# Low parts of a channel product's block operands: GpSimd in place of VectorE

## The chip, the cores and the metric

One core of one Trainium2 chip. The metric is device microseconds of the whole kernel on that core: 571.56 us is the median of three runs before the change (570.91 to 572.75).

## What is computed

A soft-capped attention over 4 batches and 12 heads, and a mixer on its output: one product along the tokens, then one along the channels.

```python
scores = scale * np.matmul(q, k.transpose(0, 1, 3, 2))
scores = cap * np.tanh(scores / cap)
attn = softmax(scores)                        # batch 4, heads 12, seq 448, head_dim 64
x = (attn @ v), heads side by side            # 4 x 448 x 768
h = np.maximum(xt @ w_tok1, 0.0) @ w_tok2     # along the tokens
u = x + h.transpose(0, 2, 1)
h2 = np.maximum(u @ w_ch1, 0.0) @ w_ch2       # along the channels, 768 -> 1536 -> 768
return u + h2
```

## The kernel before, in words

Precision comes from splitting: an operand of a large product is held as a high part (a rounded copy, `F32R`) and a low part (the operand less its high part), and each product is three matmuls, high by high, low by high and high by low (`TERMS`).

The channel product, the last 45% of the run, goes through 1536 hidden channels in `NG` = 6 groups of 256. For each group `ch1` multiplies a batch's `u` with the group's first weights into a PSUM tile, and ScalarE applies the ReLU. From group 1 on, two batches make a pair, named (group, half): (1,0), (1,1), (2,0) to (5,1), ten in all. The second product of a pair is written as seven block products of 3 x 3 matmuls each (`ch2_pair`, 63 matmuls at `L992`), which take sums and differences of the pair's hidden blocks as operands, in the manner of Strassen and Winograd. The names:

- `relu` (`L914`, ScalarE) writes two of the five buffers of `hid` for each batch. It overwrites what the pair before had there: for the first batch it waits for that pair's p4 and p2, for the second for its p5 and p3. It also frees the PSUM tile of `ch1`.
- `operands` and `form` (`L929`, GpSimd): four differences x, t1, t2 and t4 of `hid` blocks.
- `split`: for each of the seven operands p1 to p7 the high part (`L953`, ScalarE, out of `hid` into a ring of `NO` = 6 slots of `ops`) and the low part (`L958`, `hid` less the high part). A slot comes free when TensorE has read it. Products run in the order p1, p7, p6, p4, p5, p2, p3, in the last group p1, p2, p6, p7, p5, p4, p3.
- `ch2_pair`: its results accumulate in PSUM, and each product's running result is added into `u` by VectorE (`L1020` for two banks at once, `L1080` for one) before the chain's next product may write there. A ch2_pair starts when a PSUM tile of ring `a` is free, that of a ReLU of the pair behind it.
- `decode`: the next group's weights are loaded and rebuilt by VectorE and ScalarE in the same stretch: `L255` (ScalarE), `L261` and `L262`, `L268` and `L269` (VectorE); first weights then `L306` (ScalarE) and `L310` (VectorE); second weights `L281` to `L284` (VectorE, 128 columns each), `L289` and `L290` (ScalarE), `L298` and `L299` (VectorE).

TensorE does ch1 of two batches (72 matmuls) and then the ch2_pair of the pair before, in turn. So a pair's operands are made during the previous pair's ch2_pair and the next two ch1. The first pair, (1,0), has no pair before it: between its second ReLU and its ch2_pair stand two ch1 alone.

The order of each engine's instructions is fixed when the program is built: a planner (`Plan`) keeps a queue of jobs for each engine with a cost, and emits the job that could start first by its own clock. A job's cost thus sets the order of those around it. At run time each engine works strictly in that order and waits on semaphores.

`RELIEF` names the low parts that GpSimd makes. Before the change these are three, p2, p7 and p4 of the last pair (5,1); the other 67 of 70 are VectorE's.

Of the kernel before, what the change touches and what calls it, by code (L numbers as in the profile page):

```python
# [28 lines left out]
NG = FF // (GF * P)  # L29
# [20 lines left out]
    ("p3", 6, "h3", "a", 0, 1),  # L50
)
FINISH = tuple(PRODUCTS[n] for n in (0, 5, 2, 1, 4, 3, 6))
RELIEF = {(NG - 1, 1): ("p2", "p7", "p4")}

SWITCH = {("pv", "qk"): 200, ("qk", "bg"): 195, ("bg", "pv"): 147, ("qk", "pv"): 143, ("bg", "qk"): 199}
DRAIN = 250
# [49 lines left out]
class Plan:  # L106
# [27 lines left out]
    def job(self, engine, cost, took, emit, *deps, slack=0.0, key=None):  # L134
        deps += (self.pe if self.at is None else self.at,)
        j = Job(cost, took if engine in ("sp", "pool") else took + SIGNAL, emit, deps, slack)
        self.jobs[engine].append(j)
        if key is not None:
            self.done[key] = j
        return j  # L140
# [48 lines left out]
def tile_softcap_mixer(ctx, tc, qk, v, cap, w1, w2, wc1, wc2, out):  # L189
# [671 lines left out]
    while t < steps_in:  # L861
        n = 2 if PAIRED[0] <= t < PAIRED[1] else 1
# [60 lines left out]
    def operands(n, old):  # L923
        h = late["h"]
        place = {"h0": 0, "h1": 1, "t1": 2, "h3": 3, "x": 4, "t2": 0, "t4": 0}

        def form(key, out, a, b, *deps):
            e, cost = (nc.gpsimd, (1170, 1250)) if FORM == "gps" else (nc.vector, (536, 620))
            job(FORM, *cost, lambda: e.tensor_tensor(h[:, out], h[:, a], h[:, b], op=ALU.subtract),  # L929
                *deps, slack=500.0, key=("f", n, key))  # L930

        form("x", 4, 3, 2, ("r", n, 1), *([("s", old, "p7")] if old else []))
        form("t1", 2, 2, 0, ("f", n, "x"), ("r", n, 0))
        form("t2", 0, 3, 2, ("f", n, "t1"), ("s", n, "p1"))
        form("t4", 0, 1, 0, ("f", n, "t2"), ("s", n, "p6"))
        source = {"h0": ("r", n, 0), "h1": ("r", n, 0) if n[0] == NG - 1 else ("f", n, "t4"), "h3": ("f", n, "t2")}
        before = None
        for k, _, of, *_ in products(n):
            deps = [source.get(of, ("f", n, of)), room("o")] + ([("sh", n, before)] if before else [])
            split(n, k, h[:, place[of]], deps)  # L940
            before = k
# [2 lines left out]
        return FINISH if n[0] == NG - 1 else PRODUCTS  # L944

    def split(n, k, src, deps):
        on = "gps" if k in RELIEF.get(n, ()) else "dve"

        def high():
            i = len(rings["o"].holds) % NO  # L950
            t = late["o"][:, i]
            operand[n, k] = t, rings["o"].take(1)
            nc.scalar.activation(t[:, 0], src, AF.Copy)  # L953

        def low():
            t = operand[n, k][0]
            e = nc.vector if on == "dve" else nc.gpsimd
            e.tensor_tensor(t[:, 1], src, t[:, 0], op=ALU.subtract)  # L958

        job("act", 468, 568, high, *deps, slack=800.0, key=("sh", n, k))  # L960
        job(on, *((536, 620) if on == "dve" else (1170, 1250)), low, ("sh", n, k), slack=800.0, key=("s", n, k))
# [323 lines left out]
```

## Time and profile before

| | |
|---|---|
| median of three runs | 571.56 us (570.91 to 572.75) |
| profiled execution, its own time | 571.16 us |
| its span, first to last instruction | 569.4 us |
| TensorE busy | 561.8 us (99%), 3012 matmuls |
| VectorE busy | 491.4 us (86%) |
| ScalarE busy | 298.9 us (52%) |
| GpSimd busy | 61.0 us (11%) |
| chain that ended last | PE 85%, DVE 7%, ACT 3%, DMA 3% |

PE is TensorE's matmul, PEld its weight load, DVE is VectorE, ACT ScalarE, POOL GpSimd. A row of the chain is read as: start, length, what the end of the run was waiting for at that time. Where the chain shows PE, TensorE itself is what takes the time; where it shows another engine in the middle of the product, TensorE worked on something else then, but what it needed next was being made there.

### The profile page before, as it was taken

How to read it: one execution, taken by the hardware profiler on the slowest of the kernel's cores; microseconds unless marked ns; L12 is line 12 of the kernel's file. 1: busy time of each engine (PE TensorE's matmuls, PEld its weight loads, DVE VectorE, ACT ScalarE, POOL GpSimd, SP SyncE). 2: the span in 40 equal slices, each digit the busy share in tenths (PEclk: the TensorE clock that was granted, in tenths of full speed). 3: DMA queues.
4: the chain of work that ended last, by engine and by line, in shares of the span. 5: the costliest groups of instructions: out<-in, count | busy, mean ns of one | idle time of the engine just before them, and what ended most of it. 6: DMA issues, size and time to landing. Idle time of an engine off the chain costs nothing.

```text
span 569.4 us, 8201 instructions
## 1 busy us (share of the span) xinstructions
PE 561.8 (99%) x3012; PEld 431.8 (76%) x3012; DVE 491.4 (86%) x857; ACT 298.9 (52%) x415; POOL 61.0 (11%) x66
## 2 busy tenths in 40 slices
PE   8999999999999999999999999999999999999996
PEld 2333455544646799999999899999999999998995
DVE  2999999998999998637859899988999899959597
ACT  7999999899899443222234433334342424224230
POOL 0000100000000000000004202020202030303050
PEclk9999999999999999999999999999999999999999
DMA  7554767666451232000212223112220212010055
GB/s 244 174 157 117 236 193 230 208 205 203 112 167 34 70 108 75 0 2 0 75 38 74 75 55 93 37 39 74 75 69 7 83 66 75 0 39 0 3 195 193
DMA packets 26780, 55.50 MB, mean 97 GB/s; under 512 B 7024, under 2 KB 16752, under 8 KB 26736
## 3 DMA queue, kind: packets, MB, share of 16 engines
q1 hardware_dynamic: 24144, 48.21, 26.7%
q0 software_dynamic: 2160, 6.39, 3.9%
q8 instruction: 24, 0.39, 0.3%
q10 hardware_dynamic: 432, 0.34, 0.2%
q14 instruction: 20, 0.16, 0.1%
HBM read 47.97 MB, written 5.59 MB: 94 GB/s over the span
## 4 chain that ended last, share of the span: by engine, by line
PE 85%; DVE 7%; ACT 3%; DMA 3%; issue 1%; SPq 0%; DVEq 0%; ACTq 0%
PE ps_g L1033 28%; PE ps_o L992 21%; PE ps_pv L502 7%; PE ps_qk L424 6%; PE ps_h L660 6%; PE ps_u L683 5%; PE ps_o L1070 5%; PE ps_t L632 2%; PE ps_s L553 2%; PE ps_qk L435 1%; PE ps_pv L505 1%; ACT e L454 1%; DMA wraw<-in_w 1%; DVE ops L958 1%; ACT e L462 1%
## 5 line engine op out<-in xcount | busy, mean ns | idle before, releaser
L1033 PE MATMUL ps_g<-uhl,wc 128*128 128x448 f32 x648 | 137.3, 367 | 0.0
L992 PE MATMUL ps_o<-ops,wc 128*128 128x448 f32 x630 | 131.0, 367 | 0.8 <-ACT hid L914 0.5
L1033 PEld LDWEIGHTS ps_g<-uhl,wc 128*128 128x128 f32 x648 | 120.9, 188 | 11.2 <-issue 0.7
L992 PEld LDWEIGHTS ps_o<-ops,wc 128*128 128x128 f32 x630 | 117.5, 188 | 13.0 <-issue 1.3
L1080 DVE TENSOR_TENSOR u<-u,ps_o 128x448 f32<-128x448 f32 (+1 forms) x163 | 92.3, 612 | 11.0 <-PE ps_o L1070 10.6
L953 ACT ACTIVATE ops<-hid 128x448 fp32r<-128x448 f32 x70 | 38.8, 574 | 116.4 <-POOL hid L929 70.3
L454 ACT ACTIVATE e<-ps_qk,tsc 128x896 f32<-128x896 f32 x84 | 81.6, 1037 | 7.9 <-PE ps_qk L424 4.0
L929 POOL TENSOR_TENSOR hid<-hid 128x448 f32<-128x448 f32 x40 | 48.5, 1212 | 345.9 <-ACT hid L914 287.3
L462 ACT ACTIVATE e<-e,near 128x896 f32<-128x896 f32 x84 | 85.5, 1077 | 0.1
L502 PE MATMUL ps_pv<-e,vn 128*64 128x448 f32 x288 | 60.5, 549 | 0.9 <-ACT e L462 0.9
L1020 DVE TENSOR_TENSOR u<-u,ps_o 128x896 f32<-128x896 f32 x36 | 38.9, 1081 | 16.9 <-PE ps_o L992 16.9
L958 DVE TENSOR_TENSOR ops<-hid,ops 128x448 fp32r<-128x448 f32 x67 | 45.4, 694 | 1.4 <-ACT ops L953 1.4
L1033 PE MATMUL ps_g<-last_u,wc 128*128 128x448 f32 x216 | 45.3, 367 | 0.0
L502 PEld LDWEIGHTS ps_pv<-e,vn 128*64 128x64 f32 x288 | 18.0, 136 | 34.7 <-issue 24.8
L1033 PEld LDWEIGHTS ps_g<-last_u,wc 128*128 128x128 f32 x216 | 40.6, 188 | 3.8
L255 ACT ACTIVATE wz<-wraw 128x512 f32<-128x512 f32 x36 | 23.8, 672 | 28.1 <-DVE wc L310 11.3
L660 PE MATMUL ps_h<-wc,last_u 128*128 128x384 f32 x176 | 33.3, 337 | 0.0
L683 PE MATMUL ps_u<-last_u,wc 128*128 128x448 f32 x144 | 32.8, 371 | 0.0
L660 PEld LDWEIGHTS ps_h<-wc,last_u 128*128 128x128 f32 x176 | 30.8, 188 | 1.8 <-issue 1.3
L683 PEld LDWEIGHTS ps_u<-last_u,wc 128*128 128x128 f32 x144 | 26.4, 188 | 6.0 <-issue 1.8
L1070 PE MATMUL ps_o<-ops,wc 128*128 128x448 f32 x144 | 30.9, 367 | 0.0
L541 DVE TENSOR_TENSOR acc<-acc,e 64x448 f32<-64x448 f32 x48 | 29.7, 619 | 1.3
(75 smaller groups left out, 632.7 us busy)
## 6 DMA issues: line engine op xcount, KB each, us to landing
wraw<-in_wc SPq DMA_DIRECT2D x36, 512.0 KB, 3.5
qkraw<-in_qk SPq DMA_DIRECT2D x23, 448.0 KB, 4.0
vn<-in_v SPq DMA_DIRECT2D x24, 224.0 KB, 3.3
rb<-rs SPq DMA_DIRECT2D x48, 112.0 KB, 3.3
out_t<-u SPq DMA_DIRECT2D x23, 224.0 KB, 2.0
qkhi<-in_qk POOLq DMA_DIRECT2D x12, 416.0 KB, 4.3
qkhi<-qkraw POOLq DMA_DIRECT2D x3, 416.0 KB, 3.9
wraw<-in_w SPq DMA_DIRECT2D x2, 512.0 KB, 6.0
```

Of the source, the lines that this page charges most:

```text
L454: nc.scalar.activation(e, ps[:, :, :S], AF.Tanh, scale=tsc)
L462: nc.scalar.activation(e, e, AF.Exp, scale=near)
L502: nc.tensor.matmul(o, vn[x % 3][:, j * NF + c], es[b, p, c][:, j], start=first, stop=last)
L660: nc.tensor.matmul(ps[:, :HALF], w, x, start=(n == 0), stop=(n == len(mm) - 1))
L683: nc.tensor.matmul(ps[:, :S], h1[:, hi, t, cs], w2s[:, wi, t, :], start=(n == 0), stop=(n == 3 * NT - 1))
L929: job(FORM, *cost, lambda: e.tensor_tensor(h[:, out], h[:, a], h[:, b], op=ALU.subtract), *deps, slack=500.0, key=("f", n, key))
L958: e.tensor_tensor(t[:, 1], src, t[:, 0], op=ALU.subtract)
L992: nc.tensor.matmul(ps[:, :S], wblock[mc][wi][:, a], x[:, xi], start=first and m == 0, stop=m == 2, skip_group_check=not first,)
L1020: nc.vector.tensor_tensor(u[b][:, cc:cc + 2], u[b][:, cc:cc + 2], ps[:, :, :S], op=ALU.add)
L1033: nc.tensor.matmul(ps[:, i, :S], w[:, wi, cc, fs], uhl[b][:, ui, cc, :], start=(n == 0), stop=(n == 3 * NC - 1))
L1070: nc.tensor.matmul(ps[:, :S], w[:, wi, i, cs], x[:, gi, i, :], start=(n == 0), stop=(n == 3 * GF - 1))
L1080: nc.vector.tensor_tensor(u[b][:, cc, r], u[b][:, cc, r], ps[:, r], op=ALU.add)
```

## The change

`RELIEF` becomes a plain list of all seven names, and `split` asks it for every pair. All 70 low parts are then GpSimd's; for the planner such a job costs 1170 ns there in place of 536 on VectorE.

```diff
-RELIEF = {(NG - 1, 1): ("p2", "p7", "p4")}
+RELIEF = ("p1", "p7", "p6", "p4", "p5", "p2", "p3")
...
     def split(n, k, src, deps):
-        on = "gps" if k in RELIEF.get(n, ()) else "dve"
+        on = "gps" if k in RELIEF else "dve"
```

TensorE's and the DMA queue's order stays the same; VectorE's, ScalarE's and GpSimd's changes. On ScalarE, between the second ReLU of pair (1,0) and the first of pair (1,1) (`L914`), with the high parts p7, p6, p4, p5 and p2 (`L953`) and the copies of group 2's first weights (`L306`):

```order
 L255 ACTIVATE wz<-wraw 128x512 x2
-L953 ACTIVATE ops<-hid 128x448 x2
-L306 ACTIVATE wc_0_79<-wz 128x512
 L953 ACTIVATE ops<-hid 128x448
-L306 ACTIVATE wc_0_79<-wz 128x512
-L953 ACTIVATE ops<-hid 128x448
+L306 ACTIVATE wc_0_79<-wz 128x512 x2
+L953 ACTIVATE ops<-hid 128x448 x3
 L914 ACTIVATE hid<-ps_g 128x896
```

Before, p6 and p4 stood ahead of both copies and p5 between them; now both copies stand ahead of p4, p5 and p2.

On VectorE in the ch2_pair of (2,1), from the fourth product's adds on; before (`u_77` and `u_78` are the two batches, `wz` and `ws` buffers of decoding):

```order
L1080 TENSOR_TENSOR u_77<-u_77,ps_o 128x448 x4
L1020 TENSOR_TENSOR u_78<-u_78,ps_o_3665 128x896
L1080 TENSOR_TENSOR u_78<-u_78,ps_o 128x448
L958 TENSOR_TENSOR ops<-hid,ops 128x448
L1080 TENSOR_TENSOR u_77<-u_77,ps_o 128x448 x3
L958 TENSOR_TENSOR ops<-hid,ops 128x448
L1020 TENSOR_TENSOR u_78<-u_78,ps_o_3665 128x896
L1080 TENSOR_TENSOR u_78<-u_78,ps_o 128x448
L281 TENSOR_TENSOR ws<-wz 128x128
L282 TENSOR_TENSOR wz<-wz 128x128
L283 TENSOR_TENSOR ws<-ws,wz 128x128
L284 TENSOR_TENSOR ws<-wz,ws 128x128
```

and now:

```order
L1080 TENSOR_TENSOR u_77<-u_77,ps_o 128x448 x4
L281 TENSOR_TENSOR ws<-wz 128x128
L282 TENSOR_TENSOR wz<-wz 128x128
L283 TENSOR_TENSOR ws<-ws,wz 128x128
L284 TENSOR_TENSOR ws<-wz,ws 128x128
L1020 TENSOR_TENSOR u_78<-u_78,ps_o_3665 128x896
L1080 TENSOR_TENSOR u_78<-u_78,ps_o 128x448
L1080 TENSOR_TENSOR u_77<-u_77,ps_o 128x448 x3
L261 TENSOR_SCALAR wz<-wz 128x512
L262 TENSOR_SCALAR wz<-wz 128x512
L1020 TENSOR_TENSOR u_78<-u_78,ps_o_3665 128x896
L1080 TENSOR_TENSOR u_78<-u_78,ps_o 128x448
```

The low parts are gone, and six decode operations moved in among the adds, four of them ahead of the fifth product's wide add. The same move stands in the ch2_pair of (1,1) and (3,1). In the other pairs the low parts alone leave VectorE's order. GpSimd's queue is, for a pair of groups 1 to 4: the previous pair's p3, then p1, x, t1, p7, t2, p6, t4, p4, p5, p2.

## Rows read from the trace of the kernel before

**Rows 1.** The page's busy line of TensorE: busy us (share) and instructions.
```profile
PE 561.8 (99%) x3012; PEld 431.8 (76%) x3012; DVE 491.4 (86%) x857; ACT 298.9 (52%) x415; POOL 61.0 (11%) x66
```
**Rows 2.** TensorE's waits, 300 to 570 us: waiter, releaser, total, times, longest.
```profile
PE ps_o L992 <- ACT hid L914: 0.5, 1, 0.5
PE ps_o L992 <- DVE u L1020: 0.2, 1, 0.2
```
**Rows 3.** The chain that ended last, first pair and one ch2_pair: start, length, what.
```profile
302.00 0.92 ACT hid L914
...
304.82 1.56 DVE wc L298
...
313.97 1.07 DVE ops L958 x2
316.27 0.93 ACT hid L914
...
317.25 13.14 PE ps_o L992 x63
...
400.38 12.88 PE ps_o L992 x63
```
**Rows 4.** Lines L958, L929 and L1080 (317 to 560 us): count, shortest/median/longest ns.
```profile
L958 DVE TENSOR_TENSOR ops<-hid,ops x67: 612/620/1564, 302.6 to 557.5; 128x448 fp32r<-128x448 f32 x67
L958 POOL TENSOR_TENSOR ops<-hid,ops x3: 1151/1152/1154, 545.5 to 554.7; 128x448 fp32r<-128x448 f32 x3
L929 POOL TENSOR_TENSOR hid<-hid x40: 1142/1157/1537, 303.0 to 552.8; 128x448 f32<-128x448 f32 x40
L1080 DVE TENSOR_TENSOR u<-u,ps_o x127: 605/614/626, 319.8 to 559.6; 128x448 f32<-128x448 f32 x127
```
**Rows 5.** Timeline of GpSimd, 297 to 319.5 us: start, length, operation, idle time before.
```profile
303.00 4.39 POOL L929 TENSOR_TENSOR hid<-hid 128x448 f32<-128x448 f32 x3 [146.71 <-ACT hid L914]
```
**Rows 6.** Timeline of VectorE in the same stretch.
```profile
303.47 1.35 DVE L310 TENSOR_TENSOR wc<-wz,wc 128x512 fp32r<-128x512 f32 x1 [0.22 <-ACT wc L306]
...
313.28 0.69 DVE L269 SCALAR_TENSOR_TENSOR wz<-wraw,wz 128x512 int32<-128x512 int32 x1
...
314.96 0.69 DVE L310 TENSOR_TENSOR wc<-wz,wc 128x512 fp32r<-128x512 f32 x1
```
**Rows 7.** Timeline of TensorE, then of VectorE, 400 to 416 us, ch2_pair of (2,1).
```profile
400.22 13.04 PE L992 MATMUL ps_o<-ops,wc 128*128 128x448 f32 x63
...
409.57 1.08 DVE L1020 TENSOR_TENSOR u<-u,ps_o 128x896 f32<-128x896 f32 x1
...
415.29 0.29 DVE L281 TENSOR_TENSOR ws<-wz 128x128 f32<-128x128 f32 x1
```
**Rows 8.** The chain again, the last three ch2_pairs.
```profile
510.76 1.24 PE ps_o L992 x6
...
518.90 1.48 DVE ops L958
...
522.05 2.08 PE ps_o L992 x9
...
538.78 16.73 PE ps_o L992 x81
...
555.62 8.84 PE ps_o L992 x42
```
**Rows 9.** Timeline of ScalarE, 297 to 319.5 us: high parts and a decode copy.
```profile
297.55 0.56 ACT L953 ACTIVATE ops<-hid 128x448 fp32r<-128x448 f32 x1
...
314.00 0.63 ACT L306 ACTIVATE wc<-wz 128x512 fp32r<-128x512 f32 x1 [0.23 <-DVE wz L269]
314.54 0.56 ACT L953 ACTIVATE ops<-hid 128x448 fp32r<-128x448 f32 x1
```
**Rows 10.** Stretches at the end: us, engines' busy time, granted clock, DMA.
```profile
567.00:567.50 0.50, 0.00 (x0) 0.00 (x0) 0.00 (x0) 0.00 (x0) 0.00 (x0) 0.94 1.04 376
567.50:569.40 1.90, 0.00 (x0) 0.00 (x0) 0.00 (x0) 0.00 (x0) 0.00 (x0) 0.50 0.21 70
```

## The prediction

> **What bounds the kernel now.** I read the page's busy lines first, then the waits of TensorE (PE) in the stage that the change touches, then the chain of work that ended last there. TensorE is busy 561.8 us, 99% of the span [rows 1], and from 300 us on it waited for a named engine only twice, 0.5 and 0.2 us [rows 2]. The product itself runs at 12.88 us for 63 matmuls, 0.2045 us each (the piece at 400.38, [rows 3]). So a faster VectorE (DVE) or ScalarE (ACT) has almost nothing to give, and the question is where the change makes TensorE wait.
>
> Two properties of the trace answer that. First, the two engines that exchange the work disturb each other. A low part takes VectorE 620 ns in the median but up to 1564, and GpSimd (POOL) 1152 ns; a form takes GpSimd 1157 ns in the median and up to 1537 [rows 4]. Three forms in a row beside weight decoding took 4.39 us, 1.46 each [rows 5], and the VectorE subtraction that met the first took 1.35 us, where the same line alone took 0.69 [rows 6]. In the chain the two alternate: VectorE's end moves by 1.56 us there [rows 3], one GpSimd operation (1.16) plus 0.40 for the VectorE one that slips in. The adds into `u`, which read PSUM, are not touched: of 127 none took over 626 ns [rows 4], and GpSimd's forms lie among them. What collides is VectorE work with both operands in SBUF: decoding and low parts.
>
> Second, one place has no slack. The first pair (1,0) gets its second ReLU at 302.00 and its ch2_pair starts at 317.25 [rows 3]. That start needs the PSUM tile which the next pair's first ReLU frees, and this ReLU (316.27) overwrites `hid` buffers, so it needs p4's and p2's low parts (313.97, two in a row) [rows 3]. TensorE was ready 0.5 us before it ran [rows 2], at 316.76. Later pairs have a ch2_pair of 12.88 us in between, and wait for nothing there.
>
> **Part 1: 67 low parts leave VectorE, and GpSimd runs 70 instead of 3.** Removed from VectorE: 67 x 0.62 = 42 us undisturbed; added to GpSimd: 67 x 1.152 = 77 us [rows 4]. Most of both lies beside TensorE's work and costs nothing: per pair GpSimd then does 11 operations, 11 x 1.16 = 12.8 us of every 27.6. In a steady pair they follow the first read of the old operands, 9 matmuls (1.84 us) into its predecessor's ch2_pair; with p3's high and low part (1.9), 11 operations (12.8 us) and two high parts of 0.65 between them, p2, the last that a ReLU needs, is done about 17.8 us in. The ReLU has its input at 12.88 + 36 x 0.2045 = 20.2 us, and its PSUM tile is wanted at 27.6. That slack hides the longer chain; without it the pair would stall as the first one does.
>
> What is given back: TensorE lost time to VectorE's lateness twice near the end. From 510.76 to 524.13 (522.05 + 2.08) the 63 matmuls took 13.37 us [rows 8], with a wait for VectorE that ended at 522.05, the 0.2 us of [rows 2], and some held-back matmuls around it, against 12.88: 0.49. And 81 + 42 matmuls took 25.68 us from 538.78 to 564.46 against 123 x 0.2045 = 25.15: 0.53 [rows 8]. In the first case a low part of 1.48 us stood ahead of the add that ended the wait (518.90 [rows 8]); I take the second for the same. I take **-0.9**, of at most 1.0.
>
> **Part 2: the first pair.** GpSimd's queue is now p1, x, t1, p7, t2, p6, t4, p4, p5, p2, in this order (p's low parts, the rest forms). Step by step, each meeting priced as above:
> - p1's high part ends at 298.1 [rows 9]; its low runs 298.2 to 299.5, and the decoding that VectorE has there waits for it, some 0.9 us (1.56 of the step above less 0.69).
> - x 303.1 to 304.3, t1 to 305.5; p7 305.9 to 307.1 (its high part stands behind decode copies on ScalarE); t2 307.5 to 308.6, later than the 307.4 of before [rows 5]; p6's high part 0.6, then p6 309.3 to 310.5; t4 310.6 to 311.8.
> - VectorE loses about 0.9 at each meeting, and saves 0.53 for each low part gone: its last `L269` ends at 315.25 instead of 313.97 (313.28 + 0.69) [rows 6].
> - ScalarE is where it hurts. Both `L306` now stand ahead of p4's, p5's and p2's high parts, and the second waits for that `L269`. Behind it p4's high part is done 1.1 us later (as from 314.00 to 314.54 + 0.56 [rows 9]): 316.4.
> - GpSimd then needs 3 x 1.15 + 0.2 for p4, p5 and p2: 320.1. The ReLU takes 0.93 and 0.1 of signals, TensorE starts at **321.2** instead of 317.25: **+3.9**.
>
> Bounds: the trace never shows a tensor_scalar (`L261`, `L262`) beside a GpSimd operation. If these pass freely, the decoding ends 1 us sooner: +3.0. If every meeting costs VectorE its whole duration instead of 0.40: +5.0. I take 3.9, since the measured step of 1.56 is the nearest row. The Trainium skill, page "SBUF — State Buffer", section "Who interferes with whom", says that a tensor_scalar can enter a mode with two ports and then contends as well. By it the sum keeps +3.9; without it the sum would be 0.9 smaller.
>
> A stall that long may also cost clock. TensorE's last matmul ends at about 565.0 (564.46 [rows 8] and three more); the granted clock averages 0.94 of 2.4 GHz over 567.0 to 567.5 and is 0.50 (1.2 GHz) behind that [rows 10], so it fell some 2.4 us after work stopped. The new stall, from 316.76 to 321.2, is 4.4 us. If the clock falls in it and comes back as fast as it went, 2.4 us of matmuls run at half speed and lose 1.2. Between 0 and 1.2 I take **+0.6**. The Trainium skill, page "TensorE: Matmul & The Clock Gate", section "What's actually happening", says that idling brings the 1.2 GHz state; the rows agree on the fall, and no row shows a return.
>
> **Part 3: decoding moved between the adds.** With VectorE's queue shorter, the planner puts four small decode operations (`L281` to `L284`, 0.29 each [rows 7]) inside the ch2_pair of (1,1), (2,1) and (3,1), ahead of the wide add of the fifth product; before, they stood behind all adds (415.29 [rows 7]). All adds behind them wait, and for the wide add the seventh product waits. For (2,1): TensorE starts at 400.22 [rows 7], so product four ends at 407.7, and the four operations get their turn at 408.3 to 408.4. GpSimd has run without a break since p1 (404.6, after the second read at 400.22 + 18 x 0.2045 = 403.9 and p1's high part): x, t1, then p7 from 408.2 to 409.4, t2 to 410.6. `L281` waits for p7; `L282` reads what it made and waits for t2; the others slip in while GpSimd waits for p6's high part. The wide add starts at 411.2 instead of 409.57 [rows 7] and ends at 412.3. TensorE needs it at 400.22 + 54 x 0.2045 = 411.26, and gets it at 412.4. That is **+1.2** in each of three pairs, **+3.6**. Bounds for each: 0.0 (meeting none: 1.1 us of small operations fits into the gap) to 2.3 (one more meeting).
>
> **Sum.** -0.9 + 3.9 + 0.6 + 3.6 = +7.2. The profiled execution itself took 571.16, so 578.4; it lies 0.4 under the median of the three runs shown, inside their spread.
>
> **Rivals.**
> - *Faster or even:* meetings cost the path nothing, and VectorE's relief wins. For it: per pair VectorE sheds 7 x 0.62 = 4.3 us. Against: the stretched operations in the first pair [rows 3, 5, 6]. It decides at p2's low part: done by 315.7 (ReLU 0.93 and signals 0.14 ahead of 316.76), TensorE waits nowhere, and 1.0 + 0.5 us come back: 569.7.
> - *Only the first pair:* the small decode operations meet one GpSimd operation at most. For it: 0.1 us decides which engine comes first at 408.3. Against: `L282` depends on `L281`, so GpSimd gets in between. 571.16 + 3.9 + 0.6 - 0.9 = 574.8.
> - *VectorE overruns:* in the pairs with second-weight decoding, meetings with p4, p5 and p2 push the decoding past the next ch2_pair's first add, on top of the forecast, some 1.5 us in three pairs: 583. For it: each such meeting costs VectorE about 0.9. Against: low parts of 0.62 leave the same stretch.
>
> **Chances.** Forecast 0.6, only the first pair 0.2, overrun 0.12, faster or even 0.08. A measurement of this kernel tells about 0.3% (1.7 us) from no change. The forecast's own terms run from 571.16 + 3.0 - 1.0 = 573.2 to 571.16 + 5.0 + 1.2 + 6.9 - 0.9 = 583.4; with the single-place case inside and the ends of the overrun and the even case out, the range is 572.8 to 583.0. Faster by over 0.3%: 0.02 (569.7 is not quite that); within 0.3%: 0.08, most of the even case and a little of the single place; slower: 0.9.
>
> **What would show it.** Right: a wait of TensorE of some 4 us ahead of the first ch2_pair, ended by the ReLU at `L914`, with the ReLU waiting for GpSimd's `L958`; waits of about 1 us for `L1020` late in the ch2_pair of (1,1), (2,1), (3,1); no wait near 522 and 555 (plus shift); stretched `L262`, `L282`, `L269`; the granted clock below 1.00 right after the first stall. Wrong: the first ch2_pair starts near 317, or `L281` to `L284` at 0.3 us each among the adds.

## The result, and the profile after

The changed kernel takes 579.42 us (median of four runs, 578.69 to 580.16) beside 571.55 before (four runs): the medians are 7.9 us apart. The ratio estimated from the runs is 1.0127, 95% interval 1.0105 to 1.0149, which is 7.3 us slower, with 6.0 to 8.5 inside the interval. Four more runs in a later series gave 579.48 beside 571.64 (1.0125, 1.0098 to 1.0152). The forecast was +7.2, 578.4. The profiled execution took 579.84, its span is 577.7.

From the page of the changed kernel, the busy line, the granted clock in 40 slices, and the costliest line of GpSimd (busy, mean ns of one, idle before):

```profile
PE 564.5 (98%) x3012; PEld 433.6 (75%) x3012; DVE 472.6 (82%) x790; ACT 297.3 (51%) x415; POOL 138.9 (24%) x133
...
PEclk9999999999999999999999899999999999999999
...
L958 POOL TENSOR_TENSOR ops<-hid,ops 128x448 fp32r<-128x448 f32 x70 | 83.7, 1208 | 272.4 <-DVE wz L262 141.9
```

Against [rows 1] VectorE lost 67 instructions but only 18.8 us of busy time (491.4 to 472.6), where 67 low parts at their median of 0.62 [rows 4] are 41.5; GpSimd gained 78. The missing 23 us are in the main decode operations that became longer: added up, the 40 `L262` take 24.5 us in place of 17.0, and `L261`, `L268`, `L281` and `L282` 10.5 more between them. None of that would matter by itself. What matters is TensorE, and its waits from 300 us to the end of the product (waiter, releaser, total, times, longest) are these, in place of [rows 2]:

```profile
PE ps_o L992 <- ACT hid L914: 3.8, 1, 3.8
PE ps_o L992 <- DVE u L1020: 2.3, 3, 0.8
```

So there are four places, and they are the four that the prediction named. To measure them free of what lies ahead, I take the time from the second ReLU of the first pair (302.00 before [rows 3], 303.88 after) to the end of TensorE's last matmul (565.04 before, 573.47 after): 263.05 us before and 269.59 after, **+6.55**. It divides so:

| place | before | after | difference |
|---|---|---|---|
| second ReLU to the first ch2_pair's start | 15.25 | 18.52 | +3.3 |
| ch2_pair of (1,0) | 12.98 | 14.54 | +1.6 |
| ch2_pair of (1,1), (2,1), (3,1), each | 12.88 | 13.84 | +0.96, in all +2.9 |
| ch2_pair of (4,1) | 13.37 | 12.88 | -0.5 |
| last two ch2_pairs | 26.43 | 25.92 | -0.5 |

These sum to +6.8; the small rest lies in the ch1 between. The stages ahead of this stretch, whose instructions the change leaves alone but for p1's low part, begin it at 301.5 to 304.7 us in the thirteen profiles of this study, whichever the kernel. That spread is also why a single trace and the medians (+7.9) need not agree to the microsecond; +6.55 lies inside the interval.

**The first stall.** The chain of the changed kernel that ends in the first matmul of ch2_pair (1,0) (start, length, what):

```profile
316.15 0.70 DVE wz L269
...
316.88 0.03 ACT wc L306
...
317.41 0.57 ACT ops L953
...
318.05 3.36 POOL ops L958 x3
...
321.43 0.93 ACT hid L914
...
322.40 1.83 PE ps_o L992 x5
```

Read backwards: TensorE waits for the ReLU, the ReLU for three low parts in a row on GpSimd, the first of these for a high part on ScalarE, and that one stood in ScalarE's queue behind the copy `L306`, which waited for the last `L269` of the decoding. In [rows 3] the same chain ended in two low parts on VectorE at 313.97.

**The clock.** The same kernel by stretches around that start (us, engines' busy time with counts, granted clock, DMA):

```profile
322.40:322.90 0.50, 0.50 (x2) 0.48 (x3) 0.00 (x0) 0.00 (x0) 0.00 (x0) 1.00 0.00 0
322.90:326.30 3.40, 3.40 (x11) 3.00 (x11) 1.62 (x2) 0.58 (x1) 0.26 (x1) 0.50 0.00 0
326.30:330.00 3.70, 3.70 (x20) 3.40 (x19) 2.77 (x5) 1.39 (x2) 2.44 (x3) 1.00 0.00 0
```

Behind a stall of 3.8 us the granted clock was 0.50 (1.2 GHz) for 3.4 us: a matmul began every 0.37 us there, against every 0.205 in what follows at 1.00 (2.4 GHz).

**The three small stalls.** The ch2_pair of (2,1), the timeline of TensorE, then of VectorE, then of GpSimd (start, length, operation, idle time before):

```profile
407.72 11.20 PE L992 MATMUL ps_o<-ops,wc 128*128 128x448 f32 x54
419.65 2.08 PE L992 MATMUL ps_o<-ops,wc 128*128 128x448 f32 x9 [0.73 <-DVE u L1020]
```
```profile
415.95 0.86 DVE L281 TENSOR_TENSOR ws<-wz 128x128 f32<-128x128 f32 x1
416.85 1.13 DVE L282 TENSOR_TENSOR wz<-wz 128x128 f32<-128x128 f32 x1
417.90 0.28 DVE L283 TENSOR_TENSOR ws<-ws,wz 128x128 f32<-128x128 f32 x1
418.21 0.29 DVE L284 TENSOR_TENSOR ws<-wz,ws 128x128 f32<-128x128 f32 x1
418.42 1.08 DVE L1020 TENSOR_TENSOR u<-u,ps_o 128x896 f32<-128x896 f32 x1
```
```profile
415.50 1.16 POOL L958 TENSOR_TENSOR ops<-hid,ops 128x448 fp32r<-128x448 f32 x1
416.62 1.21 POOL L929 TENSOR_TENSOR hid<-hid 128x448 f32<-128x448 f32 x1
418.52 1.14 POOL L958 TENSOR_TENSOR ops<-hid,ops 128x448 fp32r<-128x448 f32 x1 [0.69 <-ACT ops L953]
```

`L281` ends 0.15 us behind p7's low part, `L282` 0.15 behind the form t2; then the other two pass at 0.28 and 0.29, the length that `L281` has in [rows 7]. The wide add comes at 418.42, 10.70 us into the ch2_pair, where it came 9.35 in before (409.57 less 400.22 [rows 7]).

### The profile page after: what moved, and what is told of

It is laid out like the page before. It is cut to its first block, busy times and chain, and to the rows that moved or that the text cites. A ratio compares the mean times of both kernels' runs of the same rounds, so it can differ in the third digit from the quotient of the medians.

```text
span 577.7 us, 8252 instructions
## 1 busy us (share of the span) xinstructions
PE 564.5 (98%) x3012; PEld 433.6 (75%) x3012; DVE 472.6 (82%) x790; ACT 297.3 (51%) x415; POOL 138.9 (24%) x133
## 4 chain that ended last, share of the span: by engine, by line
PE 77%; DVE 11%; ACT 5%; DMA 3%; issue 2%; POOL 1%; SPq 1%; DVEq 0%; ACTq 0%
PE ps_g L1033 27%; PE ps_o L992 19%; PE ps_h L660 5%; PE ps_pv L502 5%; PE ps_o L1070 5%; PE ps_u L683 5%; PE ps_qk L424 4%; ACT e L454 3%; ACT e L462 2%; PE ps_t L632 2%; PE ps_s L553 1%; DVE u L1080 1%; PE ps_pv L505 1%; DVE u L1020 1%; DMA wraw<-in_w 1%
## 5 line engine op out<-in xcount | busy, mean ns | idle before, releaser
L958 POOL TENSOR_TENSOR ops<-hid,ops 128x448 fp32r<-128x448 f32 x70 | 83.7, 1208 | 272.4 <-DVE wz L262 141.9
L992 PEld LDWEIGHTS ps_o<-ops,wc 128*128 128x128 f32 x630 | 119.2, 190 | 18.0 <-ACT hid L914 4.1
L1080 DVE TENSOR_TENSOR u<-u,ps_o 128x448 f32<-128x448 f32 (+1 forms) x163 | 91.5, 611 | 12.7 <-PE ps_o L1070 10.6
L953 ACT ACTIVATE ops<-hid 128x448 fp32r<-128x448 f32 x70 | 38.1, 573 | 103.8 <-POOL hid L929 54.1
L1020 DVE TENSOR_TENSOR u<-u,ps_o 128x896 f32<-128x896 f32 x36 | 39.1, 1085 | 36.9 <-PE ps_o L992 36.8
L929 POOL TENSOR_TENSOR hid<-hid 128x448 f32<-128x448 f32 x40 | 47.6, 1189 | 4.9 <-ACT hid L914 3.5
```

The lines of the kernel that those rows point to most:

```text
L992: nc.tensor.matmul(ps[:, :S], wblock[mc][wi][:, a], x[:, xi], start=first and m == 0, stop=m == 2, skip_group_check=not first,)
L1020: nc.vector.tensor_tensor(u[b][:, cc:cc + 2], u[b][:, cc:cc + 2], ps[:, :, :S], op=ALU.add)
L1080: nc.vector.tensor_tensor(u[b][:, cc, r], u[b][:, cc, r], ps[:, r], op=ALU.add)
```

## The experiments

All edits are made to the changed kernel. Where a stretch is named, it is again the one from the second ReLU of the first pair to TensorE's last matmul (263.05 before, 269.59 after).

**1. The first pair back on VectorE.**

```diff
-        on = "gps" if k in RELIEF else "dve"
+        on = "gps" if k in RELIEF and n != (1, 0) else "dve"
```

> The change everywhere but in the first pair (1,0), whose seven low parts stay with VectorE. My theory (two separate places): the stall ahead of the first ch2_pair is 0.5 us as before the change, no clock is lost behind it, and the waits of about 1 us each late in the ch2_pairs of (1,1), (2,1) and (3,1) stay. Sum against the kernel before: 3 x 0.95 - 1.0 = +1.9 us, so 573.4. Rival (GpSimd's extra 77 us disturb VectorE all along, and the first pair is only where it shows): most of the 7.9 us stays, over 576.

Measured 574.51 beside 572.56 (ten runs; 1.0029, 1.0015 to 1.0043): +1.95. TensorE's waits in the product:

```profile
PE ps_o L992 <- DVE u L1020: 2.2, 3, 0.7
PE ps_o L992 <- ACT hid L914: 0.5, 1, 0.5
```

The long wait is 0.5 again, the clock stays at 1.00, and the three small stalls are as they were. The first pair is a cost of its own, some 6 us by the medians (7.9 less 1.95).

**2. Only the first pair on GpSimd** (and the three low parts of the last pair that were there before).

```diff
-        on = "gps" if k in RELIEF else "dve"
+        on = "gps" if n == (1, 0) or n == (NG - 1, 1) and k in ("p2", "p7", "p4") else "dve"
```

> The change in the first pair alone (and the three low parts of the last pair, as before the change). My theory: a stall of 3.9 us ahead of the first ch2_pair instead of 0.5, and half the clock for some 3.4 us behind it, 1.6 to 1.7 us more: +5.0, so 576.5, nothing else. Rival (the changed kernel's clock fell by chance, the stall itself is the whole price): +3.4, 575.0.

Measured 577.45 beside 572.56 (1.0088, 1.0061 to 1.0116): +4.9. TensorE's waits in the product:

```profile
PE ps_o L992 <- ACT hid L914: 3.8, 1, 3.8
PE ps_o L992 <- DVE u L1020: 0.2, 1, 0.2
```

The ch2_pair of (1,0) takes 14.39, every other one what it took before, with the two stalls near the end back. Seven of the 67 operations that moved make more than half of the loss.

**3. The decoding back behind the adds.** The second-weight decoding of groups 2 to 4 is held until the last add of the ch2_pair that it had moved into, and so behind the fifth product's wide add; all low parts stay on GpSimd.

```diff
-            job("dve", 880, 870, second, (*key, 1), slack=slack, key=(*key, 2))
+            job("dve", 880, 870, second, (*key, 1), *([("o", (key[1] - 1, 1), "a", 2, 3)] if key[0] == "wc2" and key[1] in (2, 3, 4) and key[2] else []), slack=slack, key=(*key, 2))
...
-                job("dve", 4 * 190, 4 * 190 + 70, blocks, (*key, 3), ("m2",), room("ws"), slack=slack, key=(*key, 5))
+                job("dve", 4 * 190, 4 * 190 + 70, blocks, (*key, 3), ("m2",), room("ws"), *([("o", (key[1] - 1, 1), "a", 2, 3)] if key[0] == "wc2" and key[1] in (2, 3, 4) else []), slack=slack, key=(*key, 5))
```

> The whole change, but the decoding of the second weights of groups 2, 3 and 4 is held behind the last add of the ch2_pair that it had moved into; TensorE's order is that of the change. My theory (what costs there is the place in VectorE's queue, together with GpSimd's operations): the three waits of 1 us go, 579.4 - 2.9 = 576.5, and the first stall stays. Rival (the adds themselves are slowed beside GpSimd's work): the waits stay, 579.4.

Measured 576.98 beside 572.56 (1.0073, 1.0051 to 1.0096): +4.4. Every ch2_pair but the first takes 12.88, and one wait is left, the 3.8 us of the first pair. So the small stalls come from the order that the planner chose, and nothing else goes wrong when it is mended. This profile also shows the clock's fall at another size (stretches, columns as above):

```profile
320.00:325.70 5.70, 5.68 (x15) 5.08 (x16) 2.33 (x3) 0.58 (x1) 1.14 (x1) 0.50 0.00 0
325.70:330.00 4.30, 4.30 (x22) 3.94 (x22) 3.42 (x6) 1.96 (x3) 2.83 (x3) 1.00 0.00 0
```

The stall is as long as in the changed kernel (3.77 in both), but the clock was already low when TensorE began at 320.02 and stayed so for 5.7 us more: the ch2_pair took 15.56, 2.6 over the 12.98 of before, instead of 1.6.

**4. Experiments 1 and 3 together.**

> Both repairs: first pair's low parts on VectorE, and decoding held behind the adds. My theory: what is left of the change is its gain, VectorE in time at the end: 571.5 - 1.0 = 570.5, with TensorE waiting 0.5 us ahead of the first ch2_pair and nowhere else behind it. Rival (moving low parts to GpSimd costs something in every pair): above 571.5.

Measured 571.92 beside 572.56 (ten runs; 0.9985, 0.9969 to 1.0001), -0.6 where -1.0 was expected (the expectation counts from 571.5, and the kernel before took 572.56 in this series); the stretch is 0.66 shorter than before, with the gain of the last three ch2_pairs in it. Four places are the whole loss.

**5. The two copies out of the way.** On ScalarE the copies `L306` are put behind the high parts of p4, p5 and p2. No other engine's order changes.

```diff
-            job(*a, fourth, (*key, 3), *after, slack=slack, key=(*key, 4))
+            job(*a, fourth, (*key, 3), *after, *([("sh", (1, 0), "p2")] if key[0] == ("wc1", 2) and key[1] else []), slack=slack, key=(*key, 4))
```

> The changed kernel with one thing moved: on ScalarE the two copies L306 of the decode now stand behind the high parts (L953) of p4, p5 and p2 of the first pair, and no longer ahead of them; the other engines' rows stand as in the changed kernel. Theory (the first stall is a queue: the high parts wait on ScalarE behind copies that wait for a decode slowed by GpSimd, and the three low parts come only then): TensorE's wait before the first channel product is 1.2 to 2.2 us instead of 3.8, the clock may then hold, and the time is 2 to 4 us below the changed kernel. Rival (GpSimd's rate alone makes the stall, seven low parts at 1.2 us each being too many whatever stands on ScalarE): the wait stays at 3 us or more and the time within 1 us of the changed kernel.

Measured 576.48 beside 571.64 (1.0072, 1.0045 to 1.0099), 3.0 less than the changed kernel in the same series (579.48). Timelines of ScalarE, then of GpSimd, then of TensorE:

```profile
314.93 1.52 ACT L953 ACTIVATE ops<-hid 128x448 fp32r<-128x448 f32 x3 [2.81 <-POOL hid L929]
316.35 0.62 ACT L306 ACTIVATE wc<-wz 128x512 fp32r<-128x512 f32 x1
```
```profile
315.58 4.71 POOL L958 TENSOR_TENSOR ops<-hid,ops 128x448 fp32r<-128x448 f32 x3 [0.69 <-ACT ops L953]
```
```profile
321.29 7.02 PE L992 MATMUL ps_o<-ops,wc 128*128 128x448 f32 x33 [2.01 <-ACT hid L914]
```

The three high parts now wait for the form t4, their own input, and the wait of TensorE falls from 3.77 to 2.01, with the clock at 1.00 behind it. So 1.76 us of the 3.3 go with ScalarE's queue. By itself the queue held the low parts back by more: they begin 11.06 us behind the second ReLU here (315.58 less 304.52) and 14.17 in the changed kernel (318.05 less 303.88). But 1.35 of these 3.1 us are lost again: each of the three low parts now takes 1.57 instead of 1.12 (3.36 for three in the chain above), since the decoding has not ended when they run, and `L268`, `L269` and `L310` take 1.54 to 1.65 in turn with them. The meetings moved there. What is left of the stall is 1.5 over the 0.5 of before [rows 2]; experiment 6 shows whose it is.

**6. No decoding beside the first pair's last operands.** The decoding of group 2's first weights, second and third chunk, is held back until the adds of the first ch2_pair have begun.

```diff
-            job("dve", 880, 870, second, (*key, 1), slack=slack, key=(*key, 2))
+            job("dve", 880, 870, second, (*key, 1), *([("o", (1, 0), "a", 0, 0)] if key[0] == ("wc1", 2) and key[1] else []), slack=slack, key=(*key, 2))
```

> The changed kernel, with the decode of two chunks of the first channel weights of group 2 (L261, L262, L268, L269, L310, twice, and their copies L306) held back until the adds of the first channel product have begun, so that VectorE has nothing left to do beside GpSimd's last lows of the first pair. All low parts are still on GpSimd. Theory (the first stall is made by meetings of VectorE and GpSimd and by the queue on ScalarE behind the slowed decode, not by GpSimd's own 1.2 us): GpSimd's lows then take 1.15 to 1.25 us, the last ends near the time of the kernel before plus 1.4, and TensorE's first wait is 0 to 0.7 us instead of 3.8. The work is not gone: TensorE waits instead later, for L310, where the first channel weights of group 2 are read, 1.5 to 4 us. Rival (the rate of GpSimd alone makes the stall): the first wait stays at 2.5 us or more.

GpSimd's last three lows, and TensorE's waits:

```profile
314.54 3.38 POOL L958 TENSOR_TENSOR ops<-hid,ops 128x448 fp32r<-128x448 f32 x3 [0.69 <-ACT ops L953]
```
```profile
PE ps_o L992 <- DVE u L1020: 5.5, 5, 1.7
PE ps_g L1033 <- ACT wc L306: 3.6, 1, 3.6
PE ps_g L1033 <- DVE wc L310: 0.8, 1, 0.8
PE ps_o L992 <- ACT hid L914: 0.4, 1, 0.4
```

The first wait is 0.4, under the 0.5 of before: with VectorE silent beside the last operands, and ScalarE's queue free of the copies too, seven low parts on GpSimd are early enough. GpSimd's own pace does not make the first stall. The decoding is then missed elsewhere, and by more than I had said: 4.4 us for the weights of group 2 (3.6 + 0.8, with 6.8 us at half clock behind), one wait of 0.65 us in the first ch2_pair and two of 1.7 in the second, where the late decoding lies among the adds; 587.48 beside 572.01, two runs. The planner had put the decoding ahead of the first ch2_pair for a reason; there it must meet GpSimd.

**7. The clock by itself.** In the stall TensorE multiplies something that nobody reads (the rest of the edit, left out here, gives the tile of these products to the ch2_pair as its third bank).

```diff
+        spare = None
+        if n == (1, 0):
+            await_time(rings["b"].room)
+            spare = ps_b.tile([P, 512], F32, tag="b", name="ps_o"), rings["b"].take(4)
+            await_key(("s", n, "p1"))
+            await_key(("wc2", g, 0))
+            for _ in range(16):
+                nc.tensor.matmul(spare[0][:, :S], wblock[0][0][:, 0], operand[n, "p1"][0][:, 0], start=True, stop=True)
         await_time(rings["a"].room)
...
```

> The changed kernel, and TensorE does 16 extra matmuls of 128x448 (about 3.3 us, their product is thrown away) in the stall ahead of the first channel product; every other instruction stands where it stood. It prices the fall of the granted clock by itself: the products can't start sooner, since they still wait for the same ReLU. Theory (the clock fell because TensorE stood still there): the clock holds 1.00, the first channel product takes 13.0 us instead of 14.5, the time is 1.6 us (1.4 to 2.7) below the changed kernel. Rival (the fall has another cause, or costs nothing): clock at 0.50 all the same and the time within 0.5 us of the changed kernel.

Measured 577.61 beside 571.64 (1.0105, 1.0084 to 1.0127): 1.9 less than the changed kernel by the medians, 1.1 by the ratios. TensorE's timeline, then the stretches that follow:

```profile
317.73 3.43 PE L972 MATMUL ps_o<-ops,wc 128*128 128x448 f32 x16
321.73 6.57 PE L1003 MATMUL ps_o<-ops,wc 128*128 128x448 f32 x31 [0.58 <-ACT hid L914]
```
```profile
321.00:324.00 3.00, 2.42 (x12) 2.11 (x12) 0.74 (x1) 1.02 (x2) 0.00 (x0) 1.00 0.00 0
324.00:327.00 3.00, 3.00 (x17) 2.76 (x16) 2.55 (x6) 1.63 (x3) 1.95 (x2) 1.00 0.03 5
```

The products start no earlier (18.60 us behind the second ReLU, 18.52 in the changed kernel), yet the clock holds and the ch2_pair takes 12.91 instead of 14.54. The mean granted clock of the six runs is 0.998 to 1.000, where the eight runs of the changed kernel have 0.993 to 0.997. So the fall is caused by TensorE's standing still. It costs 1.6 us in the ch2_pair; the whole stretch is 1.1 shorter (268.51), as the ch1 between are some 0.4 longer in this profile, and why they are stays open.

**8. Other decode operations in the same place.** Only `L281` to `L284` are held until the last add, and so behind the wide add; the planner then puts `L261` and `L262` ahead of it.

```diff
-                job("dve", 4 * 190, 4 * 190 + 70, blocks, (*key, 3), ("m2",), room("ws"), slack=slack, key=(*key, 5))
+                job("dve", 4 * 190, 4 * 190 + 70, blocks, (*key, 3), ("m2",), room("ws"), *([("o", (key[1] - 1, 1), "a", 2, 3)] if key[1] in (2, 3, 4) else []), slack=slack, key=(*key, 5))
```

> The changed kernel, and only the four small operations L281 to L284 of groups 2 to 4 are kept behind the fifth product's wide add; the planner puts the two L261, L262 in their place ahead of it, of which each takes 0.42 us alone. Theory (any decode that stands ahead of the urgent add and meets GpSimd makes the stall, not these four): the waits of 0.7 us in the second pairs of groups 1 to 3 stay within 0.3 to 1.2 us, time within 1.5 us of the changed kernel. Rival (the four small operations are the cause): the three waits are gone and the time is 2.9 us below the changed kernel.

Measured 578.93 beside 572.01, two runs. VectorE ahead of the wide add in (2,1), and the waits for it:

```profile
415.62 1.00 DVE L261 TENSOR_SCALAR wz<-wz 128x512 f32<-128x512 f32 x1
416.66 1.26 DVE L262 TENSOR_SCALAR wz<-wz 128x512 int32<-128x512 int32 x1
417.84 1.08 DVE L1020 TENSOR_TENSOR u<-u,ps_o 128x896 f32<-128x896 f32 x1
```
```profile
PE ps_o L992 <- DVE u L1020: 1.4, 3, 0.5
```

Two operations that take 0.42 and 0.43 alone took 2.3 us, and the waits are 0.5 instead of 0.7. It is the place ahead of an urgent add that costs, whichever of these operations fills it. No run has the same place with GpSimd silent.

**9. Both orders mended, everything on GpSimd** (experiments 3 and 5 together).

> All low parts on GpSimd as in the changed kernel, with both orders mended: the copies L306 behind the high parts of the first pair, and the decode of groups 2 to 4 behind the fifth product's wide add. Theory (the costs are three separate ones that add up): only the first wait is left, 2.0 us instead of 0.5, at full clock, and the end keeps its gain: +1.5 - 1.0 = 0.2 to 1.2 us above the kernel before. Rival (GpSimd's slower low parts cost wherever they stand): 3 us or more above the kernel before.

Measured 573.61 beside 572.01 (ten runs; 1.0033, 1.0012 to 1.0054), +1.6; the stretch is 0.87 longer than before. The only wait left:

```profile
PE ps_o L992 <- ACT hid L914: 2.0, 1, 2.0
```

So the costs are separate and add up: of 7.9 us, two edits to the order alone take away 6. By the runs it is a little over the expected 0.2 to 1.2, by the trace inside. Two of the ten runs took 576.8 and 577.0 us at a mean granted clock of 0.997 and 0.995, the other eight 572.7 to 574.5 at 1.000; no trace shows where the clock fell in the two.

**10. The last group alone.**

```diff
-        on = "gps" if k in RELIEF else "dve"
+        on = "gps" if n[0] == NG - 1 else "dve"
```

> Only the low parts of the last group's two pairs, (5,0) and (5,1), are on GpSimd, the rest on VectorE as in the kernel before. Theory (what VectorE's relief gives lies in the last three channel products, and the stalls of the change lie in the first four of the second half): the stalls of 0.2 and 0.1 us in the last two stretches go, the last 26.4 us become 25.9, nothing is lost; time 0.5 to 1.1 us below the kernel before. Rival (GpSimd's low parts bring a stall near the end too): the same or slower than before.

Measured 571.02 beside 571.64 (twelve runs; 0.9986, 0.9972 to 0.9999), -0.6. Both late stalls are gone; TensorE's only wait in the product is the one ahead of the first ch2_pair:

```profile
PE ps_o L992 <- ACT hid L914: 0.5, 1, 0.5
```

The stretch is 261.80, 1.25 shorter than before. It is the best version found, with experiment 4 beside it, and its gain is at the edge of what these runs can tell.

**11. The changed kernel again.**

> The changed kernel once more, beside the other runs on this chip. Its median was 7.9 us above the kernel before, while the stretch of the trace that the change touches is longer by 6.6. If the rest is spread of the stages ahead, the difference of this run lies anywhere from 6 to 8 us and the touched stretch again between 276.5 and 278; if the change costs something ahead of it, the difference is again near 7.9 and the touched stretch starts 2 us later than before's 294.4.

Measured 579.48 beside 571.64: +7.8 by the medians, +7.2 by the ratio (1.0125). The waits are the same four, to 0.1 us, and the stretch is 269.75. The expectation counts from the first matmul of the ch1 whose ReLU begins the stretch: 294.44 before, 296.32 in the first profile of this kernel, 297.19 here; by that the touched stretch is 277.31. So both branches came true, and the run does not tell them apart.

Two things on record narrow it. The 1.9 us by which the first profile begins the stretch later (303.88 less 302.00) lie ahead of all that the change does, and 1.2 of them arise at 140 us, in the attention, where TensorE's matmuls `L553` come late; other kernels of this study show a lag at the same place. And a run's time less its span is 1.74 to 1.86 us in the 17 runs before and 2.14 to 2.21 in the eight of the changed kernel, so some 0.35 us lie outside the span; why is open. With the 6.6 to 6.7 of the stretch this gives 7.0, where the ratios say 7.2 and 7.3: the rest is far inside the intervals. One thing that can add to it in some executions is a longer time at low clock: the mean granted clock of the eight runs is 0.993 in two and 0.995 to 0.997 in the others.

## Why the prediction was right, step by step

**Part 1 (forecast -0.9, measured -1.0).** The low part ahead of an add was the cause in both late stalls: with all low parts of the last group gone from VectorE, both vanish (experiment 10). The second had been taken on analogy, which held; VectorE's timeline of the kernel before shows it, just ahead of TensorE's wait that ended at 555.62 [rows 8]:

```profile
553.21 1.26 DVE L958 TENSOR_TENSOR ops<-hid,ops 128x448 fp32r<-128x448 f32 x1
554.39 1.07 DVE L1020 TENSOR_TENSOR u<-u,ps_o 128x896 f32<-128x896 f32 x1
```

Both of these low parts had met a form on GpSimd (1.56 and 1.26 in place of 0.62), so the late stalls of before were meetings too. That the longer chain is hidden in the other pairs held as well: in the ch2_pair of (2,1) p2's low part ended 17.7 us in, forecast 17.8, and TensorE did not wait for it.

**Part 2, the stall (forecast +3.9, measured +3.3).** The steps came in the order written. GpSimd's own ran up to 0.6 us later than forecast, since the meetings stretch its operations too (t4 ended at 312.4 for 311.8); that cost nothing, as p4's high part came later still. Taking 1.88 off the times after (303.88 less 302.00), `L269` ended at 314.96 where 315.25 was forecast, p4's high part at 316.10 for 316.4, the third low part at 319.52 for 320.1, and TensorE began at 320.52 for 321.2. Two terms were too large by 0.3 each: VectorE's loss to the meetings, and the three last low parts, priced at 3.65. These had only the end of an `L310` beside them and took 3.36. Experiments 5 and 6 show the two halves: with the copies out of ScalarE's way 1.76 go, and with VectorE silent nothing is left. One of the signs did not come: `L269` was not stretched anywhere (0.72 at most); it was `L268`, ahead of it, that met (1.64 at 313.15). That `L261` and `L262` meet GpSimd at full price was the open bound; they do, and the timeline of VectorE in the first pair shows it:

```profile
309.77 1.37 DVE L261 TENSOR_SCALAR wz<-wz 128x512 f32<-128x512 f32 x1
311.18 0.43 DVE L262 TENSOR_SCALAR wz<-wz 128x512 int32<-128x512 int32 x1
...
311.98 1.25 DVE L262 TENSOR_SCALAR wz<-wz 128x512 int32<-128x512 int32 x1
313.15 1.64 DVE L268 SCALAR_TENSOR_TENSOR wz<-wraw,wz 128x512 int32<-128x512 int32 x1
```

and GpSimd's beside the last `L262`:

```profile
311.55 1.40 POOL L958 TENSOR_TENSOR ops<-hid,ops 128x448 fp32r<-128x448 f32 x1 [0.69 <-ACT ops L953]
```

The same operation takes 0.43 alone and 1.25 where it meets. The Trainium skill, page "SBUF — State Buffer", section "Who interferes with whom", has both halves of this: a tensor_scalar can enter a mode with two ports and then contends with GpSimd, and the engine that issues first holds the shared ports for its whole instruction, while the other is blocked. The trace agrees: this `L262` began 0.43 us behind GpSimd's low part and ended 0.28 behind its end (313.23 and 312.95).

**Part 2, the clock (forecast +0.6, measured +1.6).** This is the term that was mis-sized. The upper end, 1.2, came from the one fall that the trace before shows, 2.4 us behind the last matmul [rows 10], on the guess that the way back is as long. It was longer: 3.4 us at 0.50 in the changed kernel, 6.8 in experiment 3 (1.1 of it still in the stall). So the cost here runs from 1.4 (experiment 2) to 2.6. The middle of a range whose upper end was a guess was no good value; and the error was hidden. That the sum of +7.2 came so near the table's +6.8 is in part luck: the clock was rated 1.0 too low, the stall 0.6 and Part 3 0.7 too high.

**Part 3 (forecast +1.2 each, measured +0.96 each).** Place, cause and number of the stalls were right, and so were the two meetings, `L281` with p7 and `L282` with t2. The wide add began at 10.70 us into the ch2_pair, forecast was 10.98 (411.2 less 400.22). The idle time in the row (0.73) is less than the loss, since the matmul ahead of a gap is drawn longer than its turn: from its start to the next start are 1.10 us, and 0.28 to the one after that, where 0.205 is usual, so 0.97.

**The rivals.** "Only the first pair" fell with the three waits in the trace; "VectorE overruns" with the other ch2_pairs at 12.8 to 12.9 us; "faster or even" with the first stall. Its sum of 1.5 us that VectorE's relief could bring was at most 1.3 even in the kernel that has the gain alone (263.05 to 261.80 in experiment 10).

## What to carry to other kernels

Work moved to an idle engine is not judged by the busy shares of either engine, but at the places without slack: find the one operand chain that nothing covers, walk it through every queue it passes (here ScalarE's, where two unrelated copies cost 1.8 us), and look at what the planner moves into the room that came free. An operation of 0.3 us ahead of an urgent one is cheap only while nothing can hold it. Move the work where a stall of the old engine is shown and leave the rest: the 11 low parts of the last two pairs that were still VectorE's gave the whole gain; the other 56, in the order that the planner chose, only cost.

## What the runs showed that I had not expected

The clock's fall is not one price. Stalls of TensorE of 3.8 us brought it in all five profiles that have one at this place, and the one of 3.6 us in experiment 6 did too; stalls of up to 2.0 us brought it in no profile, though two of the ten runs of experiment 9, whose stall is 2.0 us, ran 3 us longer at a lower mean clock. And with the same stall of 3.77 us it began once 1.1 us ahead of TensorE's restart and once 0.5 us behind it, lasted 6.8 and 3.4 us, and cost 2.6 and 1.6. Sixteen matmuls whose results nobody reads, put into the stall, took the whole cost away (14.54 to 12.91 us).

And a decode operation's price is set by its neighbour: `L282`, 128 columns, took 1.13 us beside GpSimd, 3.9 times its 0.29 alone, and `L262` 2.9 times (1.25 to 0.43), while `L1020`, seven times as wide as `L282` but with one operand in PSUM, took 1.08 at 418.42 with GpSimd's low part of 418.52 at work beside it.
